# Releasing one weight load behind the first copy, with two warm-up matmuls and one filler fewer

## The chip, the cores and the metric

The kernel runs on one core of a Trainium2 chip. The metric is the device time of one execution in microseconds (us), the median of several; the execution that was profiled also gives a span, some 1.7 us shorter, on which all times of the traces below are counted. A load is issued when its instruction starts on the queue of an engine, and has landed when its semaphore shows that all of its bytes are in.

## The reference, cut to what matters

Two branches on the same x (2048 x 512, bf16), mixed by a gate: attention in four segments with a carried memory, and a gated feed-forward. Only the very first work matters here: Q, K and V of the first segment.

```python
q = (x @ wq).reshape(B, S, H, Dh)...     # H = 32, Dh = 16
k = (x @ wk).reshape(B, S, H, Dh)...
v = (x @ wv).reshape(B, S, H, Dh)...
# per segment: softmax attention plus memory read-out; then
return g * (attention @ wo) + (1 - g) * (relu(x @ W_gate) * (x @ W_up)) @ W_down
```

## The kernel before

All work is listed as operations with estimated lengths, a small scheduler puts them in one fixed order per engine, and each is then emitted. The change leaves that order alone. The parts concerned (cuts marked by `...`):

```python
    def c_dummy(e):                        # warm-up of TensorE, on a tile of ones
        for _ in range(31):
            nc.tensor.matmul(g_dummy.t[:, 0:P], lhsT=ones, rhs=ones, start=True, stop=True)
    ...
    x0_part(0, 0, "SP", -300)              # first half of the columns of x, two row halves
    x0_part(0, 1, "ACT", -300)
    wq_part(0, 1, "ACT", -299)
    x0_part(1, 0, "SP", -299)
    x0_part(1, 1, "POOL", -110)
    wq_part(1, 2, "POOL", -95)             # the later parts of wq: from GpSimd's queue
    wq_part(2, 4, "POOL", -80)
    ...
    lw["wk"] = loadw("wk", wk_sb, A_wk, 0, D, 1)          # SyncE's queue, then wv, gate_w, beta, gate, up ...
    o_wk0 = op("wk0", {"DVE": 0.08}, lambda e: nc.vector.memset(wk_sb[0:1, 0, 0:1], 0.0), key=-600, cls=0)
    lw["wk"].deps.append((o_wk0, None))                    # the load overwrites it, so it has to wait for it
    ...
    def first_x(c, after):                 # transpose x on TensorE, copy it out: half 0 VectorE, half 1 ScalarE
        ...
                if e == "DVE":
                    nc.vector.tensor_copy(dst, gv)
                else:
                    nc.scalar.activation(dst, gv, ACT.Copy)
    ...
    first_x(0, None)
    first_x(1, None)
    for ci in range(NC):
        def f(e, ci=ci):
            if ci == 0:
                for _ in range(3):         # fillers while the first copies run
                    nc.tensor.matmul(qS.t[:, 0, 0:P], lhsT=ones, rhs=ones, start=True, stop=True)
            for c in range(NC):            # one contraction block of Q
                nc.tensor.matmul(qS.t[:, c, :], lhsT=wq_sb[:, ci, c * P:(c + 1) * P], rhs=xT[0].t[:, ci, :], ...)
        ...
        if ci < 2:
            first_x(ci + 2, o_q0)
    o_wk0.deps.append((xc0[0][0], None))
```

The one-element memset in wk is a gate: it keeps wk's 512 KB off the DMA engines while x and wq come in. TensorE's queue runs in this order: warm-ups, 8 transposes, fillers, Q block 0, 4 transposes, Q block 1, 4 transposes, Q blocks 2 and 3, then K, V, the first gate products and the first attention scores.

The softmax here doesn't subtract the row's maximum and nothing guards it: scores larger than these inputs give would overflow.

## Time and profile before

| | |
|---|---|
| time, median of the first 3 runs (all) | 265.79 us (265.42 to 266.17) |
| span of the profiled execution | 263.9 us (its time 265.61) |
| TensorE busy | 257.2 us, 97% |
| the chain that ended last | TensorE 97% |

The chain is followed back from the last instruction to what released it, so it says which engine or transfer sets the end. Its lines and those of the first 10 us are in the prediction and are read there.

### The profile page before, as it was taken

Reading aid. Unit: us, or ns where it says so; the run is one execution under the profiler, and the core shown is the slowest. Engines: PE = TensorE matmul, PEld = TensorE weight load, DVE = VectorE, ACT = ScalarE, POOL = GpSimd, SP = SyncE. Lnnn points to the kernel's source line nnn. Section 1 sums busy time; section 2 is a strip of 40 time slices with the busy share of each in tenths; the row PEclk is TensorE's granted clock in tenths of the full one; section 3 lists DMA queues with packets and bytes.
Section 4 is the critical chain, followed back from the end, with each engine's and each line's share of the span. In section 5 each row is a group of like instructions: output and inputs, shape, how many; then the busy total and the mean of one; then the engine's idle time right before and its main releaser. Section 6 shows DMA issues by size and latency. Waiting matters only on the chain.

```text
span 263.9 us, 7083 instructions
## 1 busy us (share of the span) xinstructions
PE 257.2 (97%) x2817; PEld 116.7 (44%) x2850; DVE 183.8 (70%) x411; ACT 194.7 (74%) x189; POOL 175.6 (67%) x436
## 2 busy tenths in 40 slices
PE   8999999999999999999999999999999999999995
PEld 7444444444444443443444444444444444434454
DVE  1488978889878938798789278794977271665452
ACT  3599699988879568989786578987888576787302
POOL 8418177869788888475479788884577885474600
PEclk9999999999999999999999999999999999999999
DMA  6997159522332310200703010000003000100002
GB/s 163 290 246 173 41 173 266 127 82 79 93 108 45 92 41 1 62 2 0 180 5 96 0 43 20 22 1 0 2 15 80 22 4 5 39 20 2 0 2 80
DMA packets 27761, 17.96 MB, mean 68 GB/s; under 512 B 14032, under 2 KB 27088, under 8 KB 27728
## 3 DMA queue, kind: packets, MB, share of 16 engines
q1 hardware_dynamic: 27136, 16.72, 25.0%
q0 software_dynamic: 176, 0.52, 0.6%
q8 instruction: 22, 0.36, 0.6%
q10 hardware_dynamic: 416, 0.26, 0.3%
q14 instruction: 11, 0.09, 0.1%
HBM read 9.84 MB, written 2.10 MB: 45 GB/s over the span
## 4 chain that ended last, share of the span: by engine, by line
PE 97%; issue 1%; DVE 0%
PE G L275 75%; PE S L785 9%; PE G L897 7%; PE G L273 2%; PE S L456 1%; PE G L317 1%; PE G L658 1%; PE G L432 0%; PE G L834 0%; DVE os L746 0%; PE S L454 0%
## 5 line engine op out<-in xcount | busy, mean ns | idle before, releaser
L809 POOL TENSOR_SCALAR_AFFINE_SELECT E<-E 64x256 bf16<-64x256 bf16 x256 | 116.2, 454 | 62.6 <-ACT E L799 49.4
L799 ACT ACTIVATE E<-S 128x2048 bf16<-128x2048 f32 x72 | 135.0, 1876 | 30.1 <-PE S L785 28.7
L275 PE MATMUL G<-xT,wg_sb 128*128 128x512 bf16 x202 | 54.7, 380 | 0.9 <-issue 0.5
L275 PE MATMUL G<-xT,wu_sb 128*128 128x512 bf16 x205 | 54.7, 380 | 0.2
L275 PE MATMUL G<-wd_sb,hT 128*128 128x512 bf16 (+2 forms) x242 | 53.2, 355 | 1.0 <-issue 0.6
L710 DVE TENSOR_TENSOR hT<-G,os 128x512 bf16<-128x512 f32 x56 | 38.3, 685 | 18.6 <-ACT os L706 8.0
L932 DVE STREAM_TRANSPOSE T<-G 128x512 f32<-128x512 f32 x44 | 29.4, 698 | 14.1 <-PE G L897 13.0
L706 ACT ACTIVATE os<-G 128x512 bf16<-128x512 f32 x56 | 33.0, 595 | 5.9 <-PE G L275 5.1
L275 PEld LDWEIGHTS <-hT 128*128 128x128 bf16 x252 | 22.4, 98 | 23.9 <-issue 2.6
L275 PEld LDWEIGHTS <-wu_sb 128*128 128x128 bf16 x208 | 19.2, 98 | 24.1 <-issue 3.0
L275 PEld LDWEIGHTS <-wg_sb 128*128 128x128 bf16 x212 | 19.3, 98 | 23.4 <-issue 2.6
L785 PE MATMUL S<-QT,K 32*128 32x192 bf16 (+7 forms) x512 | 28.6, 287 | 0.1
L785 PEld LDWEIGHTS <-K 32*128 32x128 bf16 x512 | 8.2, 92 | 29.8 <-issue 29.2
L746 DVE TENSOR_SCALAR os<-G,ngcol 128x512 bf16<-128x512 f32 (+2 forms) x10 | 6.4, 644 | 20.7 <-PE G L275 20.6
L897 PE MATMUL G<-E,Vp 64*32 64x128 bf16 (+7 forms) x512 | 18.8, 284 | 0.0
L897 PE MATMUL G<-E,VS 64*32 64x128 bf16 (+7 forms) x512 | 18.4, 284 | 0.0
L748 ACT ACTIVATE os<-G,ngcol 128x512 bf16<-128x512 f32 x8 | 5.5, 687 | 16.4 <-PE G L275 16.4
L275 PE MATMUL G<-wo_sb,oT 128*128 128x512 bf16 (+2 forms) x70 | 17.3, 355 | 0.2 <-issue 0.2
L275 PE MATMUL G<-wv_sb,xT 128*128 128x512 bf16 x63 | 15.8, 380 | 0.1
L275 PE MATMUL G<-xT,wk_sb 128*128 128x512 bf16 x60 | 15.6, 380 | 0.1
L952 DVE TENSOR_TENSOR O<-T,sm 128x256 bf16<-128x256 f32 x32 | 15.4, 519 | 0.2
L529 POOL COPY R<-rcol 32x4 f32<-32x4 f32 x64 | 13.3, 208 | 3.1
(93 smaller groups left out, 285.4 us busy)
## 6 DMA issues: line engine op xcount, KB each, us to landing
VS<-Vp SPq DMA_DIRECT2D x8, 296.0 KB, 3.6
out_dram<-os SPq DMA_DIRECT2D x15, 128.0 KB, 1.7
xn<-in_A_x_dram SPq DMA_DIRECT2D x3, 512.0 KB, 4.7
wd_sb<-in_B_W_down_dram SPq DMA_DIRECT2D x3, 512.0 KB, 3.5
wg_sb<-in_B_W_gate_dram SPq DMA_DIRECT2D x2, 512.0 KB, 5.9
wu_sb<-in_B_W_up_dram SPq DMA_DIRECT2D x2, 512.0 KB, 6.5
wg_sb<-in_B_W_gate_dram SPq DMA_DIRECT2D x3, 256.0 KB, 5.9
wu_sb<-in_B_W_up_dram SPq DMA_DIRECT2D x3, 256.0 KB, 6.2
```

The source lines that it names most:

```text
L275: nc.tensor.matmul(out_ap, lhsT=lhsT, rhs=rhs, start=start, stop=stop)
L529: nc.gpsimd.tensor_copy(R[s][32 * j:32 * j + 32, k, :], rcol[32 * k:32 * k + 32, cols])
L706: nc.scalar.activation(rg.t[:], g.t[:], ACT.Relu)
L710: nc.vector.tensor_tensor(h.t[:], u.t[:], rg.t[:], ALU.mult)
L746: nc.vector.tensor_scalar(ob.t[:, cs], g.t[:, 0:W], ngcol[:, tt:tt + 1], None, ALU.mult)
L748: nc.scalar.activation(ob.t[:, cs], g.t[:, 0:W], ACT.Copy, scale=ngcol[:, tt:tt + 1])
L785: nc.tensor.matmul(sp.t[:, j, off:off + w], lhsT=K2[s, cc].t[rows, kb, :, :].rearrange("p r k -> p (r k)"), rhs=QT[s, cc].t[rows, L - w:L] ...
L799: nc.scalar.activation(eb_.t[:], sp.t[:], ACT.Exp, scale=SCALE)
L809: nc.gpsimd.affine_select(out=v, in_=v, compare_op=ALU.is_ge, fill=0.0, base=0, pattern=[[0, 4], [1, 64]], channel_multiplier=-1)
L897: nc.tensor.matmul(gs[r].t[32 * j:32 * j + 32, L - w:L], lhsT=v, rhs=src.t[rows, j, off:off + w], start=(kb == 0), stop=(kb == 7), tile_po ...
L932: nc.vector.transpose(T.t[:].rearrange("p b e -> p (b e)"), g.t[:])
L952: nc.vector.tensor_tensor(O.t[:, :, r, :], T.t[:, :, 0:DH], sm.t[:, r, :, None].to_broadcast([P, 16, DH]), ALU.mult)
```

## The change

The intent: start Q sooner by taking out idle warm-up work, and let wk's load start sooner so that it keeps up with Q.

```diff
-        for _ in range(31):
+        for _ in range(29):
             nc.tensor.matmul(g_dummy.t[:, 0:P], lhsT=ones, rhs=ones, start=True, stop=True)
...
-    o_wk0 = op("wk0", {"DVE": 0.08}, lambda e: nc.vector.memset(wk_sb[0:1, 0, 0:1], 0.0), key=-600, cls=0)
+    o_wk0 = op("wk0", {"DVE": 0.08}, lambda e: None, key=-600, cls=0)
...
                     nc.vector.tensor_copy(dst, gv)
+                    if (c, h) == (0, 0):
+                        nc.vector.memset(wk_sb[0:1, 0, 0:1], 0.0)
...
-                for _ in range(3):
+                for _ in range(2):
                     nc.tensor.matmul(qS.t[:, 0, 0:P], lhsT=ones, rhs=ones, start=True, stop=True)
```

## The prediction

> **What bounds the kernel now.** I read the page first, then the chain that ended last for the first 20 us, then the timeline of the first 14 us (again in stretches of half a microsecond, to part merged instructions), then the DMA issues one by one. From the page:
>
> ```profile
> span 263.9 us, 7083 instructions
> ...
> PE 257.2 (97%) x2817; PEld 116.7 (44%) x2850; DVE 183.8 (70%) x411; ACT 194.7 (74%) x189; POOL 175.6 (67%) x436
> ...
> PE 97%; issue 1%; DVE 0%
> ```
>
> TensorE is busy for 97% of the span, and the chain that ended last is TensorE for 97% of it. So a microsecond is won only if TensorE has less to do, does it at a faster clock, or starts real work sooner. The change touches only the start, so the start has to be read. The chain there, in order of time (start, length, what):
>
> ```profile
> 0.83 3.46 PE G L317 x31
> 4.29 0.85 PE G L432 x8
> 5.15 0.32 PE S L454 x3
> 5.47 1.15 PE S L456 x4
> ...
> 7.93 1.73 PE S L456 x8
> 9.65 4.32 PE G L275 x20
> ```
>
> L317 is the warm-up (31 matmuls on ones), L432 the transposes of x, L454 the three fillers, L456 the Q projection, L275 the K projection and everything dense after it. The chain never leaves TensorE: one kind of work follows the other with nothing between. The timeline has what stands beside it (start, length, engine, line, operation; in brackets the idle time before and its end):
>
> ```profile
> 0.83 3.46 PE L317 MATMUL G<-const-bfloat16-1.0 128*128 128x128 bf16 x31 [0.83 <-PEq L1059]
> 3.98 0.89 PEld L432 LDWEIGHTS <-xn 128*128 128x128 bf16 x8
> 4.76 0.51 DVE L440 COPY xT<-G 128x256 bf16<-128x256 bf16 x2 [3.38 <-PE G L432]
> 5.20 0.06 DVE L377 MEMSET wk_sb<- 1x1 bf16 x1
> 5.26 1.35 PE L456 MATMUL S<-xT,wq_sb 128*128 128x512 bf16 x4
> 5.32 0.37 SPq L373 DMA_DIRECT2D wk_sb<-in_A_wk_dram  x1
> 5.69 0.15 PEld L456 LDWEIGHTS <-wq_sb 128*128 128x128 bf16 x1 [0.28 <-issue]
> 6.02 0.10 PEld L456 LDWEIGHTS <-wq_sb 128*128 128x128 bf16 x1 [0.18 <-issue]
> ...
> 9.32 1.99 PEld L275 LDWEIGHTS <-wk_sb 128*128 128x128 bf16 x10 [0.17 <-DMA wk_sb<-in_A_wk_dram]
> 9.49 2.32 PE L275 MATMUL G<-xT,wk_sb 128*128 128x512 bf16 x10
> ```
>
> Three things are to be seen. First, the clock: Q's matmuls start at 5.26, 5.69, 6.02, 6.24 us, so 0.43, 0.33 and then 0.22 us apart. The array doubles its rate inside the second one: with x us of the 0.33 at the slow rate, x/0.427 + (0.33-x)/0.216 = 1 gives x = 0.23, that is at 5.92 us. Second, wk: its load is issued at 5.32, behind the memset at 5.20, and its first use waits for the landing at 9.32. Third, that wait costs nothing yet: the last four Q matmuls run from 8.63 to 9.66, the last starts at 9.28, and the first K matmul comes 0.21 us later, at the ordinary spacing. wk lands exactly in time.
>
> The issues, with the size and the microseconds from issue to landing:
>
> ```profile
> xn<-in_A_x_dram ACTq DMA_DIRECT2D x1, 128.0 KB, 3.0
> wq_sb<-in_A_wq_dram ACTq DMA_DIRECT2D x1, 128.0 KB, 3.5
> wk_sb<-in_A_wk_dram SPq DMA_DIRECT2D x1, 512.0 KB, 4.0
> ```
>
> The x part that the first transposes need is issued at 0.79 and lands at 3.8; wq's first part (issued 1.30) lands at 4.8.
>
> **What the Trainium skill says.** "TensorE: Matmul & The Clock Gate", Part 1 (The HAM clock gate): an idle array runs at half clock, start to start 106.7 ns for 128 columns and 426.7 for 512, and 55.6 and 215.7 once warm; the trace agrees (31 warm-ups in 3.46 us with 0.43 and 0.22 us above). It also says that a free-running window of some 3.4 us of activity, and not a number of matmuls, releases the clock, so the moment differs from run to run. The trace shows one such moment, 5.92 us; that it moves is not shown. The view's granted clock reads 1.00 from the start and does not show the slow phase; the spacing decides. "DMA: Bandwidth & Descriptors", Anatomy of one DMA: the wait for a semaphore is at the issuing queue, ahead of dispatch, and each DMA has a fixed cost of about 2 us. The trace agrees in kind: the DMA engines are idle from about 6.85 and busy again from 7.3, so wk's bytes move 2.0 us after its issue, and 2.0 more bring 512 KB in. So an earlier memset moves the landing by the same amount.
>
> **The change, part by part.**
>
> *Two warm-ups fewer.* Each is a slow 128-column matmul, 0.107 us; two are 0.214 us of TensorE. The next work, the weight load of the first transpose, stood at 3.98 and could now stand at 3.77. But its x lands at 3.8, so x takes over as the wait and the transposes move up by about 0.17, not 0.21. They finish 0.17 earlier, and so do the copies behind them.
>
> *One filler fewer.* Another 0.107. The fillers cover the time until the first copies of x are in. The first VectorE copy runs 4.76 to 5.05 now, and will run 4.59 to 4.88. Behind two fillers Q could start at 5.26 - 0.17 - 0.107 = 4.98: after the copy by 0.1 us, and after wq's landing at 4.8. So nothing new waits, and Q starts 0.28 us sooner.
>
> *What that is worth.* The 0.28 us is gained before 5.92, at the slow rate: 0.28/0.427 = 0.65 of a 512-column matmul. If the clock rises at the same moment, TensorE is full from there on, and those 0.65 matmuls no longer have to be done at the fast rate: 0.65 x 0.216 = 0.14 us. This is the gain when the clock rises in Q, as in this profile; it is half of what the counts suggest.
>
> *The memset moved.* It ran behind the second VectorE copy (the third x copy counting ScalarE's), 0.23 us behind that copy's start at 4.97. Behind the first one, at 4.59, it stands at 4.82, and wk is issued 0.12 later, at 4.94 instead of 5.32: 0.38 earlier, of which 0.17 from the warm-ups and 0.21 from the move. Landing at 4.94 + 4.0 = 8.94. Q now wants it at 9.28 - 0.14 = 9.14, so wk is off the path with 0.2 us to spare. Without the move it would land at 9.15, again only just. Of itself the move gains nothing in this profile: it protects the 0.14. The second copy is pushed back by some 0.06 to 0.1 us behind the memset; it is read by the second block of Q at 6.7, so this lies beside other work. All later loads of that queue (wv, gate, up) are issued up to 0.4 us earlier; no one waited for them.
>
> *Sum.* 0.14 us in this clock phase. Where the clock rises earlier than 5.92, Q ends earlier and wk, not TensorE, sets the start of K in the kernel before; there the gain goes up to wk's 0.38. I take 0.2 us as the mean. All behind 9.5 us hangs on TensorE and moves up with it: 265.79 - 0.2 = 265.6.
>
> **The rivals.**
>
> *The clock sets everything.* If the clock rises before Q in most executions, wk is the real wait of the kernel before and the gain is 0.3 to 0.4 us: 265.4. For it: wk is only just in time already. Against it: the single profile has the rise at 5.92, and times of before spread by 0.75 us, more than this whole effect.
>
> *x takes over and the slack is gone.* x lands at 3.8 with no margin; where it lands 0.1 or 0.2 later, the removed warm-ups are replaced by idle time, and only the filler and the move are left: 0.05 to 0.1 us, 265.7. Against it: the landing has its queues to itself at that time.
>
> *The gap delays the clock.* With less activity ahead of it, the rise could come later; every microsecond of that costs 0.5 us of work: up to 266.5. For it: fewer matmuls in the window. Against it: the gap is some 0.04 us in over 5 us of unbroken work.
>
> *Instruction supply.* TensorE has six instructions fewer (three matmuls with their weight loads), so the small gaps marked "issue" (1% of the span) fall elsewhere: perhaps 0.2 us either way, spread over the kernel.
>
> **Range and chances.** The largest mechanism here is worth 0.4 us, 0.15% of the time; 2% is 5.3 us, and nothing touched is that big. The range is mainly noise: 265.42 to 266.17 in three runs of before, so 0.4 about the middle, widened for the rivals: 265.0 to 266.2. Within 2%: 0.98; the rest is for a wait that I have not seen.
>
> **What would show it.** Right: 29 warm-ups, the first transpose load at about 3.8 and waiting for x; two fillers; Q's first matmul at 4.95 to 5.0; wk's memset at 4.8, its issue at 4.9 and landing at 8.9 to 9.0; K's first weight load without a wait for DMA; K's first matmul near 9.35 if the spacing of Q halves near 5.9, earlier if sooner. Wrong: Q starting after 5.1 (a copy, wq or x late), a wait for wk still ahead of K, the slow spacing lasting beyond 6.5 us, or the 0.14 us gone by 30 us into another engine's wait.

## The result, and the profile after

| | before | changed |
|---|---|---|
| median of 6 runs each | 265.93 us | 265.86 us |
| range | 265.40 to 266.35 | 265.32 to 266.19 |
| ratio | | 0.9998 (0.9979 to 1.0017) |

A ratio is the mean time of one kernel's fast runs over that of the other's in the same rounds, so not quite the ratio of the medians quoted; the range behind it is a 95% interval. The median is near the forecast, but the profiled execution of the changed kernel does not look as forecast: its span is longer, and a transfer has come into the chain. From the page of the changed kernel:

```profile
span 264.4 us, 7077 instructions
...
PE 95%; DMA 2%; issue 1%; DVE 0%
```

The chain of the changed kernel in order of time (start, length, what):

```profile
0.83 3.25 PE G L317 x29
...
4.55 0.34 DVE xT L440 x2
4.89 5.05 DMA wk_sb<-in_A_wk_dram
9.95 0.05 issue
9.99 4.49 PE G L275 x20
```

Where before TensorE's own work ran through from 0.83 to the end, the chain now leaves TensorE for the first copy and its memset, and then sits for 5 us in the load of wk. The timeline of the changed kernel, the lines that answer to those in the prediction:

```profile
0.83 3.25 PE L317 MATMUL G<-const-bfloat16-1.0 128*128 128x128 bf16 x29 [0.83 <-PEq L1061]
3.80 0.82 PEld L432 LDWEIGHTS <-xn 128*128 128x128 bf16 x8
3.88 0.91 PE L432 MATMUL G<-ident,xn 128*128 128x128 bf16 x8
4.55 0.50 DVE L440 COPY xT<-G 128x256 bf16<-128x256 bf16 x2 [3.17 <-PE G L432]
4.78 0.06 DVE L442 MEMSET wk_sb<- 1x1 bf16 x1
4.89 0.37 SPq L373 DMA_DIRECT2D wk_sb<-in_A_wk_dram  x1
4.99 1.02 PE L458 MATMUL S<-xT,wq_sb 128*128 128x512 bf16 x4
9.99 1.84 PEld L275 LDWEIGHTS <-wk_sb 128*128 128x128 bf16 x10 [1.43 <-DMA wk_sb<-in_A_wk_dram]
9.99 2.33 PE L275 MATMUL G<-xT,wk_sb 128*128 128x512 bf16 x10 [0.94 <-DMA wk_sb<-in_A_wk_dram]
```

Up to 4.99 us everything stands within 0.05 us of the forecast: the weight load of the transposes at 3.80 (3.8), memset at 4.78 (4.82), issue at 4.89 (4.94), Q at 4.99 (4.98). Then two things differ. Q's four matmuls take 1.02 us instead of 1.35: the array had doubled its rate at about 4.50 us, during the transposes, against 5.92 in the trace before, so the last Q matmul starts at 8.67 instead of 9.27. And wk, issued 0.43 us earlier than before, lands at 9.95, that is 0.67 us later, so TensorE stands idle for 0.94 us. K starts at 9.99 instead of 9.49.

All behind it is the same. The busy times from the first attention score (13.90 us before, 14.41 in the changed kernel) to the end, before and then changed (stretch, its length, then busy us and instructions of each engine, clock, DMA share, GB/s):

```profile
13.90:264.00 250.10, 244.16 (x2733) 108.28 (x2764) 179.49 (x390) 188.26 (x177) 167.49 (x420) 1.00 0.24 59
```

```profile
14.41:264.40 249.99, 244.38 (x2733) 108.31 (x2764) 179.14 (x388) 188.25 (x177) 165.97 (x420) 1.00 0.24 59
```

From the first score the rest takes 250.0 us in both; in all fourteen traces it took 249.9 to 250.2. So the whole question is when that first score starts, and it starts 4.4 us behind K where nothing waits in between. A time of 265.4 means K at about 9.3 us, one of 266.4 K at about 10.3.

### The profile page after: what moved, and what is told of

Read it like the earlier page. It is cut to its first block, busy times and chain, and to the rows that moved or that the text cites. A ratio compares the mean times of both kernels' runs of the same rounds, so it can differ in the third digit from the quotient of the medians.

```text
span 264.4 us, 7077 instructions
## 1 busy us (share of the span) xinstructions
PE 256.9 (97%) x2814; PEld 116.0 (44%) x2847; DVE 184.2 (70%) x411; ACT 194.8 (74%) x189; POOL 174.0 (66%) x436
## 3 DMA queue, kind: packets, MB, share of 16 engines
HBM read 9.84 MB, written 2.10 MB: 45 GB/s over the span
## 4 chain that ended last, share of the span: by engine, by line
PE 95%; DMA 2%; issue 1%; DVE 0%
PE G L275 75%; PE S L787 9%; PE G L899 7%; PE G L273 2%; DMA wk_sb<-in_A_wk_dram 2%; PE G L317 1%; PE G L660 1%; PE G L836 0%; PE G L432 0%; DVE os L748 0%; DVE xT L440 0%
## 5 line engine op out<-in xcount | busy, mean ns | idle before, releaser
L899 PEld LDWEIGHTS <-Vp 64*32 64x32 bf16 x512 | 12.2, 91 | 6.2 <-issue 3.4
```

Source lines behind the costliest of these rows:

```text
L899: nc.tensor.matmul(gs[r].t[32 * j:32 * j + 32, L - w:L], lhsT=v, rhs=src.t[rows, j, off:off + w], start=(kb == 0), stop=(kb == 7), tile_po ...
```

## The experiments

**The theories.** Theory 1, from the two traces: wk's landing, and not TensorE, sets the start of K in most executions of both kernels. Its rival: the wait for wk is chance in the one profiled execution, and the rest is noise. After four runs I formed Theory 2: the landing does not follow the issue, because the loads share the DMA engines, and the clock's rise differs by chance from one execution to the next.

What all the runs gave, in one table. "Rise" is where the spacing of TensorE's instructions halves in the trace, read to some 0.02 us; last Q is the start of the last Q matmul, K is the first K matmul, S the first attention score; times in us.

| run | rise | wk issued, landed | last Q | K | S | mean of the runs | ratio to before (95%) |
|---|---|---|---|---|---|---|---|
| before | 5.92 | 5.32, 9.28 | 9.27 | 9.49 | 13.90 | 265.90 (39 runs) | |
| changed | 4.50 | 4.89, 9.95 | 8.67 | 9.99 | 14.41 | 265.81 | 0.9998 (0.9979 to 1.0017) |
| after_again | 4.84 to 4.99 | 4.89, 9.23 | 8.67 | 9.28 | 13.70 | 265.82 | 0.9999 (0.9979 to 1.0019) |
| after_kq | 6.20 | 4.89, 9.03 | 9.25 | 9.47 | 14.12 | 265.90 | 0.9999 (0.9975 to 1.0022) |
| before_kq | 3.64 | 4.86, 9.37 | 8.52 | 8.74 | 13.31 | 265.52 | 0.9984 (0.9972 to 0.9996) |
| after_late | 3.99 | 5.95, 10.06 | 8.50 | 10.11 | 14.53 | 266.35 | 1.0016 (1.0004 to 1.0027) |
| after_split | 3.77 | 4.59, 9.43 and 10.30 | 8.46 | 9.48 | 15.03 | 266.40 | 1.0015 (0.9996 to 1.0034) |
| warm_only | 6.69 | 5.14, 9.84 | 9.51 | 9.88 | 14.31 | 265.68 | 0.9993 (0.9978 to 1.0009) |
| memset_only | 5.70 | 5.11, 9.43 | 9.17 | 9.48 | 13.90 | 265.57 | 0.9989 (0.9974 to 1.0005) |
| after_wvgate | 5.44 | 4.89, 8.96 | 8.88 | 9.10 | 14.96 | 266.08 | 1.0004 (0.9985 to 1.0023) |
| after_early | 5.99 | 1.82, 9.58 | 14.61 | 15.04 | 20.04 | 270.30 | 1.0156 (1.0128 to 1.0185) |
| after_actgate | 3.60 | 3.48, 8.05 | 10.36 | 10.57 | 14.99 | 266.65 | 1.0030 (1.0013 to 1.0047) |
| act_swap | 6.14 | 3.48, 8.87 | 10.67 | 10.88 | 15.30 | 266.71 | 1.0032 (1.0014 to 1.0051) |
| wq_on_act | 3.73 | 4.58, 10.62 | 8.85 | 10.66 | 15.08 | 265.61 | 0.9979 (0.9965 to 0.9993) |

The instruction order of every engine was the same as in the kernel altered, but for the instructions named.

### after_kq and before_kq: K of the first segment from wq

Wrong on purpose (both were still within the tolerance of the comparison), so that nothing waits for wk; its load stays.

```diff
-        a = dense(f"k{s}{c}", g, lambda ci: wk_sb[:, ci, c * P:(c + 1) * P], ...
+        a = dense(f"k{s}{c}", g, lambda ci: (wq_sb if s == 0 else wk_sb)[:, ci, c * P:(c + 1) * P], ...
```

> The changed kernel with the K projection of segment 0 computed from wq instead of wk (wrong result on purpose; the load of wk stays as it is), so that nothing waits for wk's landing. Theory 1 (wk's landing sets the start of K in most executions of both kernels): K starts right behind Q, at 8.9 us where the clock rises before Q and near 9.35 where it rises in it, against 9.3 to 10.2 that the times of the changed kernel imply; V may then wait 0.1 to 0.3 us for wv. So 0.3 to 0.8 us faster than the changed kernel, about 265.3 us. Rival (wk binds only in an odd execution such as the profiled one, the rest is noise): within 0.1 us of the changed kernel.

> The kernel before with the same K from wq. Theory 1: it too is 0.3 to 0.8 us faster than with wk, and 0.14 to 0.3 us slower than the changed kernel with K from wq, which is what the warm-ups and the filler are worth where wk hides nothing. Rival: within 0.1 us of the kernel before.

The kernel before became 0.16% faster, some 0.4 us, and the interval leaves out 1, narrowly (0.9996), as one of thirteen such intervals here. So the wait for wk probably costs the kernel before something in its ordinary executions, although its one trace shows none. In the trace of before_kq K follows Q at once:

```profile
8.74 2.32 PE L275 MATMUL G<-xT,wq_sb 128*128 128x512 bf16 x10
```

The changed kernel did not become faster (265.90 mean), though Theory 1 expected 0.3 to 0.8 us. Its runs spread from 264.88 to 267.21, and in its trace the next load is what TensorE waits for, wg's first part, landed at 13.54 us against 12.43 before:

```profile
13.58 0.11 PEld L275 LDWEIGHTS <-wg_sb 128*128 128x128 bf16 x2 [0.56 <-DMA wg_sb<-in_B_W_gate_dram]
```

So Theory 1 is supported for the kernel before, and is too narrow for the changed one: behind wk stand wv and wg in the same queue, and they can hold TensorE as well. The second half of the forecast for before_kq also missed: it was to be 0.14 to 0.3 us slower than after_kq, and its mean is 0.4 us lower (265.52 against 265.90).

### after_late: the changed kernel with a longer gate

```diff
-                    if (c, h) == (0, 0):
-                        nc.vector.memset(wk_sb[0:1, 0, 0:1], 0.0)
+                    if (c, h) == (1, 0):
+                        nc.vector.memset(wk_sb[:].rearrange("p c n -> p (c n)"), 0.0)
```

> The changed kernel with the memset over the whole of wk and behind the second VectorE copy: wk is issued some 0.6 to 1.0 us later, at 5.5 to 5.9 us. Theory 1 with a fixed time from issue to landing (4.0 to 5.0 us): 0.6 to 1.0 us slower than the changed kernel, about 266.7. Theory 1 with a landing that hangs on the transfers of wq still in flight and not on the issue: the time to landing shrinks to 4.0, the landing stays at 9.5 to 9.9, and the kernel is 0 to 0.2 us slower. Rival (wk not binding): 0 to 0.3 us slower, and K's first weight load waits for wk in the trace.

wk was issued 1.06 us later than in the changed kernel and the mean rose by 0.54 us. A fixed time to landing would have cost the whole; no dependence, nothing. The trace:

```profile
10.11 2.33 PE L275 MATMUL G<-xT,wk_sb 128*128 128x512 bf16 x10 [1.23 <-DMA wk_sb<-in_A_wk_dram]
```

This time the load took 4.1 us, and the five times lie within 0.19 us (266.24 to 266.43), where the changed kernel's twelve spread over 1.3 us. With wk as the only thing that is waited for, and issued at 5.95 when only the last part of wq (in at 6.37) was still under way, even the times are steady. That the spread of the other kernels comes from the start as well is suggested by these five times, not shown.

### after_split: wk by two loads

```diff
-    lw["wk"] = loadw("wk", wk_sb, A_wk, 0, D, 1)
+    def f(e):
+        for c0 in (0, 2):
+            nc.sync.dma_start(out=wk_sb[:, c0:c0 + 2, :], in_=wview(A_wk)[:, c0:c0 + 2, :])
+    lw["wk"] = load("wk", f, P * NC * D * 2, 1)
```

> The changed kernel with wk loaded by two DMAs of 256 KB, the contraction blocks 0 and 1 first. Theory 1: K's first two matmuls need only the first half, which lands up to 0.7 us before the whole; the next two wait for the second half, so at most 0.43 us is won: 0.2 to 0.4 us faster than the changed kernel. Rival: within 0.1 us.

Not faster but some 0.6 us slower than the changed kernel in the mean, which is barely clear of the noise (its ratio to the kernel before is not clear of 1). In its trace TensorE waits three times, for the two halves and for wv:

```profile
9.48 0.60 PE L275 MATMUL G<-xT,wk_sb 128*128 128x512 bf16 x2 [0.64 <-DMA wk_sb<-in_A_wk_dram]
10.35 1.90 PE L275 MATMUL G<-xT,wk_sb 128*128 128x512 bf16 x8 [0.26 <-DMA wk_sb<-in_A_wk_dram]
12.78 1.89 PE L275 MATMUL G<-wv_sb,xT 128*128 128x512 bf16 x8 [0.54 <-DMA wv_sb<-in_A_wv_dram]
```

The first half, issued at 4.59, took 4.8 us for 256 KB: more than the whole of wk took in the kernel before.

### after_again, warm_only, memset_only: the change once more, and its parts

after_again is the changed kernel unaltered; warm_only has the two numbers (31 to 29, 3 to 2) and the memset left in its old place; memset_only has the memset moved and the numbers left.

> The changed kernel unaltered, for more times and a second trace. Theory 2, formed on the first four runs: the DMA stage sets the start; wk's landing stays at 9.0 to 10.0 us whether it is issued at 4.6 or at 5.3, because an earlier issue meets the last packets of wq and is soon shared with wv, and the moment at which the clock rises differs from execution to execution (3.6 to 6.2 us in the traces so far) but only sets the start of K where it is late. So 265.5 to 266.2 as before, with a wait for wk at K where the rise is before 5 us. Rival (the late landing in the first trace of the changed kernel was chance, the normal landing is 8.9): wk lands at 8.8 to 9.1 and TensorE does not wait for it by over 0.2 us.

> The kernel before with the two warm-ups and the filler taken out and the memset left where it was. Theory 2: within 0.15 us of the kernel before, 265.9; wk is issued 0.1 to 0.2 us earlier and lands at 9.0 to 9.8. The prediction: 0.1 to 0.15 us faster. A wait for wk of over 0.2 us at K where the clock rises before 5 us speaks for Theory 2.

> The kernel before with the memset moved behind the first copy, warm-ups and filler left. Theory 2: the landing does not move with the issue: wk issued at 4.9 to 5.1 lands at 9.2 to 10.0, later loads land no earlier than before (wv 10.8 to 11.6), and the time is within 0.15 us of the kernel before. Rival (landing = issue + 4.0): lands at 8.9 to 9.1 and the kernel is 0.2 to 0.3 us faster.

No ratio of the three is clear of 1: 0.9999, 0.9993, 0.9989. So the times do not decide between the theories: memset_only's mean lies 0.3 us below the kernel before, which is what its rival expected. The landings do. In the second trace of the changed kernel wk lands at 9.23, 0.72 us earlier than in the first at the same issue, and TensorE still waits for it:

```profile
9.28 2.33 PE L275 MATMUL G<-xT,wk_sb 128*128 128x512 bf16 x10 [0.23 <-DMA wk_sb<-in_A_wk_dram]
```

memset_only issued wk 0.21 us earlier than the kernel before did and landed 0.15 us later (9.43); K started at 9.48, as before. warm_only landed it at 9.84. Both rivals (landing at 8.8 to 9.1 in after_again, at 8.9 to 9.1 in memset_only) fall for these traces. The sign named for warm_only, a wait at a rise before 5 us, could not be tried: its rise came at 6.69.

Four more traces with a rise after the start of Q and no wait inside it, beside the trace before, also size the TensorE part of the change by itself. In the slow phase half the work is done, so the start of the last Q matmul less half the rise should be one number for each count of warm-ups:

| | warm-ups | last Q - rise/2 |
|---|---|---|
| before | 31 | 9.27 - 2.96 = 6.31 |
| memset_only | 31 | 9.17 - 2.85 = 6.32 |
| after_kq | 29 | 9.25 - 3.10 = 6.15 |
| warm_only | 29 | 9.51 - 3.35 = 6.16 |
| after_wvgate | 29 | 8.88 - 2.72 = 6.16 |

The warm-ups and the filler bring 0.16 us at an equal, late rise. With an early rise they bring nothing, as far as one pair of traces shows: 8.52 with 31 warm-ups (before_kq, rise 3.64) and 8.50 with 29 (after_late, rise 3.99). In both TensorE stands idle between the last filler and Q, for 0.24 and 0.31 us: Q comes behind VectorE's first copy and the landing of wq's first part, and work that is taken out ahead of them comes back as idle time.

### after_wvgate: the later loads held back

```diff
+                    if (c, h) == (1, 0):
+                        nc.vector.memset(wv_sb[:].rearrange("p c n -> p (c n)"), 0.0)
```

> The changed kernel with wv, and with it all later loads of that queue, held back until a memset over the whole of wv behind the second VectorE copy, so that wv is issued at 5.7 to 6.0 instead of 5.3 while wk still goes at 4.7 to 4.9. If wk is late because wv's packets share the engines with it: wk lands at 8.6 to 9.0, K starts behind Q, and the kernel is 0.2 to 0.5 us faster than the changed one unless wv (landing then at 11.2 or later) takes the wait over. If wk is late because of wq's packets still under way at its issue: wk lands at 9.2 to 10.0 all the same and the kernel is as fast as the changed one or 0.1 to 0.3 us slower.

wv was issued at 6.16 instead of 5.30, and wk landed 4.07 us after its issue, at 8.96, the earliest of all kernels that release it at 4.6 us or later. K followed Q. But the wait moved on, to the gate's first part:

```profile
9.10 2.32 PE L275 MATMUL G<-xT,wk_sb 128*128 128x512 bf16 x10
14.42 0.60 PE L275 MATMUL G<-xT,wg_sb 128*128 128x512 bf16 x2 [1.28 <-DMA wg_sb<-in_B_W_gate_dram]
```

The time was no better (1.0004). That the sharing with wv is what delays wk is not shown by it: after_kq, which shares, landed wk at 9.03.

### after_early, after_actgate, act_swap: a much earlier release

after_early puts the memset among VectorE's first ones; after_actgate replaces it by a one-element ScalarE copy into wk behind ScalarE's warm-up; act_swap also issues the first gate and up loads ahead of gate_w and beta.

```diff
         nc.vector.memset(mcole[:], 0.0)
+        nc.vector.memset(wk_sb[0:1, 0, 0:1], 0.0)                              # after_early
...
         nc.scalar.activation(scratch[:], ones[:, 0:1], ACT.Exp)
+        nc.scalar.activation(wk_sb[0:1, 0, 0:1], ones[0:1, 0:1], ACT.Copy)     # after_actgate, act_swap
...
+    lgw.emit, lwg[0].emit, lwu[0].emit = lwg[0].emit, lwu[0].emit, lgw.emit    # act_swap
```

> The changed kernel with the memset among the first ones of VectorE (at 1.0 us), so that wk is issued behind x, at 1.8 us, and its bytes run against the later parts of x and wq. Theory 2 (the start is set by the DMA stage: the sum of the bytes and not wk's issue): wk lands by 6 to 7 us and no longer holds K, but the parts of wq land 0.5 to 1.5 us later than their 5.5 and 6.7, Q waits for them and ends at 9 to 10; K starts at 9.0 to 10.0 and the time is within 0.5 us of the changed kernel either way. Simple theory (each load lands a fixed time behind its issue): K starts right behind Q at 8.9 to 9.4, the times of the other loads move up by 3 us, and the kernel is 0.4 to 0.7 us faster.

> The changed kernel with wk released by a one-element ScalarE copy behind its warm-up, at some 3.5 us instead of 4.8, so that wk's bytes fill the engines while the last parts of wq are being taken in. Theory 2 with room left in the engines (they stand partly idle from 4.0 to 7.3 us in the traces): wk lands at 7.5 to 8.7, the last part of wq at 6.5 to 7.3, K starts behind Q at 8.9 to 9.4, and the kernel is 0.2 to 0.5 us faster. Theory 2 without room (wq and wk share what there is): wk lands at 8.7 to 9.5, wq's last part after 7.3, and the kernel is as fast as the changed one within 0.2 us.

> The same, and the first gate and up parts are issued ahead of the broadcast of gate_w and of beta, which are needed later. Theory 2: where K no longer waits, the first gate part (12.4 to 13.5 us so far, wanted at 12.8 to 13.4) is the next load that can hold TensorE; issued two places sooner it lands 0.5 to 0.9 us sooner. So 0 to 0.3 us faster than the version without the swap, and no wait for wg in the trace. If nothing waited for wg: the same within 0.1 us.

All three are slower, after_early by 1.6%. K no longer waits for wk, but Q waits for x or wq. From the traces of after_early and after_actgate:

```profile
7.95 0.29 PE L433 MATMUL G<-ident,xn 128*128 128x128 bf16 x2 [1.35 <-DMA xn<-in_A_x_dram]
...
11.65 3.59 PE L457 MATMUL S<-xT,wq_sb 128*128 128x512 bf16 x8 [0.71 <-DMA wq_sb<-in_A_wq_dram]
```

```profile
8.84 1.90 PE L457 MATMUL S<-xT,wq_sb 128*128 128x512 bf16 x8 [1.68 <-DMA wq_sb<-in_A_wq_dram]
```

In after_early wq's last part landed at 11.60 instead of 6.53, and wk, issued 3.5 us sooner than in the kernel before, at 9.58, later than there. Eight Q matmuls took 3.59 us where they take 1.90: after those waits the array ran slow again. This shows that wk's bytes, released early, hold back those of x and wq. "DMA: Bandwidth & Descriptors", Issuing engines are not separate DMA queues, says the same: transfers issued by several engines run on the same 16 DMA engines and interleave. Both of my variants of the expected gain were too hopeful; of after_actgate's, wk's landing (8.05) was right, and wq's (8.79 against 6.5 to 7.3) was what failed. The swap brought nothing, as the first gate part, landing at 11.48, was not waited for.

### wq_on_act: the later parts of wq from ScalarE's queue

```diff
-        o = first_load(f"wq{c0}", eng, key, 131072 * (c1 - c0), lambda: wq_sb[:, c0:c1, :],
-                       A_wq[c0 * P:c1 * P, :].rearrange("(c p) n -> p c n", p=P))
+        o = first_load(f"wq{c0}", eng, key, 131072 * (c1 - c0), None, None)
+        o.emit = lambda e: [nc.scalar.dma_start(out=wq_sb[:, a:b, :], ...) for a, b in ((0, 1), (1, 2), (2, 4)) if c0 == 0]
```

> The changed kernel with the two later parts of wq issued from ScalarE's queue straight behind the first part, from 1.8 us, instead of from GpSimd's at 2.8 and 3.4 us; all else, and every order on the other engines, as it is. If wk's landing behaves as it does because wq's GpSimd-issued parts are still under way when wk is issued: all of wq is in by 5.0 to 5.8 us, wk (issued at 4.8 to 5.0) lands 4.0 us later at 8.7 to 9.0, Q is not held, K starts at 8.9 to 9.5 and the kernel is 0.2 to 0.5 us faster than the changed one, 265.5. If it behaves so for another reason (the start-up of a load, the sharing with wv): wk lands at 9.2 to 10.0 and the time is within 0.2 us of the changed kernel. It can also be that x is held up by the earlier wq: then Q starts after 5.3 and the kernel is up to 0.5 us slower.

The mean is 0.2% below the kernel before, with an interval clear of 1 (0.9965 to 0.9993), and one execution took 264.94 us. Yet the profiled one was its slowest, 266.66, and it contradicts the reason for the try: wq was in no sooner (6.19 and 6.86), and wk took 6.0 us, the longest of all that were released near 5 us:

```profile
10.66 2.33 PE L275 MATMUL G<-xT,wk_sb 128*128 128x512 bf16 x10 [1.43 <-DMA wk_sb<-in_A_wk_dram]
```

The lag is not one of bytes. What SyncE's queue (q1), of which wk is the first load here, had moved from 4.5 to 9.0 us in the kernel before and in wq_on_act (packets, MB, share of 16 engines):

```profile
q1 hardware_dynamic: 649, 0.65, 52.9%
```

```profile
q1 hardware_dynamic: 778, 0.78, 62.4%
```

wk is 0.52 MB. More had been moved than in the kernel before, where wk landed at 9.28, but bytes of wv were among them and wk was not complete until 10.62. "DMA: Bandwidth & Descriptors", Why a DMA increments its semaphore by 16 and not by 1, says that one DMA runs on up to 16 engines that finish independently and has landed only with the last; the trace fits that, but does not say which engine was behind, nor why.

What the packed traces also hold, though no view of `prof` prints it, is the time of each of the 16 increments of a load's semaphore, here called its shares (read from the landings in trace.npz). For the ten traces that load wk at once and issue it between 4.58 and 5.95 us:

| run | wk issued | issue to its eighth share | issue to its last | its first share to its last | the same of wq's last part |
|---|---|---|---|---|---|
| before | 5.32 | 3.80 | 3.97 | 0.30 | 0.37 |
| changed | 4.89 | 4.10 | 5.05 | 1.65 | 0.83 |
| after_again | 4.89 | 3.95 | 4.34 | 1.20 | 0.95 |
| after_kq | 4.89 | 3.73 | 4.14 | 0.76 | 0.61 |
| before_kq | 4.86 | 4.16 | 4.52 | 0.68 | 0.67 |
| after_late | 5.95 | 3.81 | 4.11 | 0.49 | 0.50 |
| warm_only | 5.14 | 3.84 | 4.70 | 1.15 | 0.67 |
| memset_only | 5.11 | 3.90 | 4.33 | 0.60 | 0.28 |
| after_wvgate | 4.89 | 3.96 | 4.07 | 0.63 | 0.41 |
| wq_on_act | 4.58 | 3.83 | 6.03 | 2.63 | 1.29 |

Half of wk is in 3.7 to 4.2 us after the issue, in every one of them: so far the landing does follow the issue. The last share does not: it came 0.1 to 2.2 us behind the eighth, and TensorE waits for it. In wq_on_act the first share of wv was in at 9.38, 1.2 us ahead of wk's last. Where the shares of wq's last part came in far apart, those of wk mostly did too (correlation 0.91 over the ten). That fits some engines being behind already with wq and still behind with wk; as the increments do not name their engine, it is not shown.

## Why the prediction was right or wrong

- **That the time would hardly move: right.** Forecast 265.6 us in 265.0 to 266.2, measured 265.86. Over twelve runs the changed kernel's mean is 265.82 against 265.90 in 39 runs of before, a difference of 0.1 us with an uncertainty of some 0.27 us (95%, from the two standard deviations of 0.43 and 0.32 us). The forecast gain of 0.2 us is neither seen nor ruled out: no change at all would have fitted the forecast as well, so the number says nothing for the mechanism. It was also lucky, as an earlier Q and a later wk partly cancelled (K at 9.99 and 9.28 in the two traces, 9.49 before).
- **Warm-ups and filler: the size held, two steps of its working did not.** At an equal late rise they are worth 0.16 us, forecast 0.14. x was to take over as the wait and cost 0.04 us. It landed at 3.75, and the transposes start at 3.88, right behind the last warm-up, where the trace before has 4.09: they moved by the whole 0.21. Only in warm_only, where that part of x landed at 3.89, did TensorE wait for it, 0.06 us. And "nothing new waits" was wrong: Q's first weight load, at 4.96, comes 0.12 us behind the end of VectorE's first copy (4.84). At a late rise this costs under 0.05 us, and Q's start at 4.99 (forecast 4.98) owes something to the two errors cancelling. With an early rise TensorE stands idle there, 0.25 us in the changed kernel's first trace, and the 0.16 us is gone (8.52 against 8.50); this case was missing.
- **"If the clock rises at the same moment": it does not.** The rise fell between 3.60 and 6.69 us in fourteen traces. The trace before, with 5.92, was taken as typical; nine of the other thirteen were earlier. The prediction named the varying rise, but took its mean effect from the idea that an early rise lets wk's 0.38 us count.
- **"So an earlier memset moves the landing by the same amount": this is the step that failed.** The memset and the issue came 0.05 us ahead of the forecast (4.78, 4.89), the landing did not come at 8.94 but at 9.95 and 9.23, and "a wait for wk still ahead of K", which the prediction had named as a sign of being wrong, stands in both traces (0.94 and 0.23 us). Released between 4.58 and 5.32 us, wk landed between 8.96 and 10.62, with no order in the issue. The forecast 4.0 to 4.1 us were met in before, after_late, after_kq and after_wvgate; the other seven traces with a release near 5 us took 4.3 to 6.0. What failed is the end of the load: in the ten traces that load wk at once half of its shares do come 3.7 to 4.2 us behind the issue, the last up to 2.2 us later. I had carried the 4.0 us of one load, whose 16 shares landed within 0.30 us, over to loads whose shares came in up to 2.6 us apart. The split of the 4.0 us was misread as well: SyncE's queue, of which wk is the first load there, moved 40 packets of 1 KB from 6.32 to 6.83 us, before the pause of 6.85 to 7.3 whose end the prediction took for the first of wk's bytes.
- **"No one waited for" the later loads: true of the trace before and of both traces of the changed kernel, not of every variant.** In before_kq, after_kq and after_wvgate TensorE waited for the gate's first part, in after_split for wv.
- **The rival "wk is the real wait of the kernel before" was more right than I gave it credit for.** Taking the wait away gained 0.16% in the kernel before, narrowly clear of noise. But it does not follow that an earlier issue takes it away.

What stays open: what holds back the last shares of a load, by up to 2 us, when it is released while wq is still coming in; and whether wq_on_act's 0.2% has its cause in the start at all, as its only trace shows a slow execution.

## What to carry to other kernels

When a load is only just in time in one trace, ask for a second trace before building on its slack: here its landing moved by 0.7 us between two executions of one kernel. A load lands with the last of its 16 shares, so a time to landing from one trace is that of its slowest share there. Releasing a load earlier is a gain only while the transfers ahead of it leave room; else it takes from them what it wins, and with a run of loads in one queue the wait just moves to the next. An effect of 0.16 us on TensorE is not to be seen through a start that varies by 1 us; it can be sized in the traces, by comparing executions at the same clock phase.

## What the Trainium skill lacked or had wrong

- "TensorE: Matmul & The Clock Gate", Part 1: it puts the transition about 4 us into the activity, 0.5 us either way. Here it came 2.8 to 5.9 us after the first matmul (at 3.60 to 6.69 us, the first matmul at 0.83), with 29 or 31 warm-ups alike. That the moment is a matter of chance agrees with the page.
- The same page, Part 4, says that the full clock does not engage for transposes on TensorE. In the changed kernel's trace the transposes of x start 0.107 us apart up to 4.41 us and 0.056 apart from 4.52 us on, the same two figures as plain matmuls of that width. The kernel calls `nc.tensor.transpose` for them; whether these matmuls against the identity are in the mode that the page means, the trace does not say.
- "DMA: Bandwidth & Descriptors", Anatomy of one DMA: its fit (2.0 us and the bytes at 436 GB/s) is for loads issued by GpSimd and has no term for other loads under way; as an estimate it would give 3.2 us for 512 KB. wk, issued by SyncE near 5 us, took 4.0 to 4.1 us at best and up to 6.0.
- No page has that a load's time to landing scatters so between executions of one kernel at the same issue: 5.1 and 4.3 us, both issued at 4.89; nor how far the 16 shares of one load come in apart: 0.30 to 2.63 us here.
